# First row block on centered rows, its factor applied to the hidden units; fewer warm products, w1 loaded behind them

## The chip, the cores and the metric

The kernel runs on one core of a Trainium2 chip. The core has a matrix engine (TensorE, PE in the profile; the loading of its stationary operand is PEld), a vector engine (VectorE, DVE), a scalar engine for functions and copies (ScalarE, ACT), a fourth engine (GpSimd, POOL) and one that here only issues transfers (SyncE, SP). Each engine takes its instructions in the order written, and waits at one until its operands are there. Transfers between memory and the chip run on 16 DMA engines. The metric is the device time of the run in microseconds, as a median of several runs.

## The reference

x has 2048 rows of 640. The reference normalises each row, xn = (x - mean) / sqrt(var + 1e-5), and returns the sum of three things:

```python
a = jnp.einsum("bsd,ed->bse", xn, dft_hid_re)
b = jnp.einsum("bsd,ed->bse", xn, dft_hid_im)
y = jnp.einsum("ts,bse->bte", dft_seq_re, a) - jnp.einsum("ts,bse->bte", dft_seq_im, b)
h = gelu(jnp.einsum("bsd,df->bsf", xn, w1) + b1)      # 640 -> 1536, tanh form
m = jnp.einsum("bsf,fd->bsd", h, w2) + b2             # 1536 -> 640
return x + y + m
```

The part that the change touches is the first product of the two-layer network, xn times w1, for the first 512 rows.

## The kernel before

Every product is made in a split form: an operand is written as a high part in a rounded 32-bit format and a low part, the rest, and three products (high with high, high with low, low with high) stand for one. A split costs one copy on ScalarE (the high part, line 160) and one subtraction on VectorE (the low part, line 161).

The rows are worked on in blocks of 512 (`TB`). A hidden *unit* is 128 of the 1536 columns of w1, so a block has 12 units (`NF`). For a unit, `hidden(g)` (line 289) makes 5 x 3 products of 128x128 by 128x512 into one of three banks, `gelu(g, acc)` (line 310) applies bias and Gelu on ScalarE (314), copies the high part (318) and subtracts for the low part on VectorE (320), and `output(g)` (line 322) makes 5 x 3 products (lines 277 to 279) that add the unit's share to five output banks. The loop from line 1003 writes these out by hand: for the first block, at g, the weights of the next units are split (`prep_w1`, `prep_w2`), further ones are loaded, `first_block(i)` (886) does a piece of the normalising of later rows, and then come `hidden(g+2)`, `gelu(g+2)`, `output(g)`. The two-layer network of the later blocks and the Fourier part follow behind; nothing of them is changed.

Before the loop stands the head (lines 633 to 724), where nearly all of the waiting of TensorE for data lies. It loads four row tiles x0 to x3 of 128 rows (`load_x`, SP's queue), and then the weights in the same queue. VectorE zeroes a tile and casts it to three `warm` tiles. These lie in the three buffers that later hold the first three units of w1 (tag `w1r`), and so the load of a unit of w1 has to wait until the last product on the warm tile in its buffer is done. `NWARM` is the number of products on warm tiles, `NGATE` the numbers at which they go from one warm tile to the next: of 19, the first 7 use the first tile, 3 the second, the other 9 the third. Their result is not used.

Meanwhile the rows are normalised. The statistics of x0, x2 and x3 are made on VectorE (`ln_stats`, 185 and 186), of x1 on ScalarE (672 to 678). `ln_scale` (188) makes the factor, 1 / sqrt(var + eps): a Sqrt on ScalarE (192) and five small steps on VectorE. With mean and factor the rows are written, transposed in blocks of 32 columns, into `xp` (x0 and x1 on ScalarE, 686; x2 and x3 on VectorE, 208). TensorE transposes `xp` by 128x128 into five banks (`transpose_x`, 667), one for each 128 of the 640 columns; each bank takes a piece from each of the four row tiles. Five splits make the moving operands `XT[j]` of it. Between the rows, the first unit of w1 is split (706 and 711). `FIRST` (307) is the order of the 15 products of unit 0, by the column block j and the kind k (0 high-high, 1 high-low, 2 low-high): it follows the order in which the splits finish.

Some lines that a sentence can't say as shortly:

```python
NWARM = 19
NGATE = (7, 10)
    for k in range(NWARM):
        warm = warms[sum(k >= n for n in NGATE)]
        nc.tensor.matmul(wacc, warm[:, :P], warm, start=True, stop=True)
```

Of the kernel before, what the change touches and what calls it, by code (L numbers as in the profile page):

```python
# [19 lines left out]
NWARM = 19  # L20
NGATE = (7, 10)
TAIL = 4
PADL = 8
# [3 lines left out]
def kernel(  # L27
# [78 lines left out]
    def bank(k):  # L106
        return banks[:, k]
# [181 lines left out]
    def hidden(g):  # L289
# [9 lines left out]
        for n, (j, k) in enumerate(steps):  # L299
            a, b = kinds[k]  # L300
            nc.tensor.matmul(  # L301
                acc, W1[i][:, a, j * P : (j + 1) * P], XT[j][:, b], start=n == 0, stop=n == len(steps) - 1
            )
# [3 lines left out]
    FIRST = [(0, 0), (1, 0), (0, 2), (1, 2), (2, 0), (2, 2), (0, 1), (3, 0), (3, 2)]  # L307
    FIRST += [(1, 1), (4, 0), (4, 2), (2, 1), (3, 1), (4, 1)]

    def gelu(g, acc, fill=lambda k: None):  # L310

        i = unit(g)
        a = AB[:, g % 2]
        nc.scalar.activation(a, acc, AF.Gelu_apprx_tanh, bias=b1c[:, i : i + 1])
# [6 lines left out]

    def output(g):
        t, i = divmod(g, NF)
        if i == 0:
            oacc[t] = [bank(3 + e) for e in range(ND)]
        second(t, i, unit(g), HT[g])
# [305 lines left out]

    for c in range(NC):
        load_x(c)
    nc.gpsimd.memset(eps, EPS)
# [10 lines left out]
    for k in range(NWARM):  # L646
        warm = warms[sum(k >= n for n in NGATE)]
        nc.tensor.matmul(wacc, warm[:, :P], warm, start=True, stop=True)
    load_w1(2)
    load_w2(0)  # L650
    nc.sync.dma_start(b1c, b1.rearrange("(i p) -> p i", p=P))
    load_w2(1)
    load_w2(2)
# [16 lines left out]
    m = MV[:, 1]  # L670
    scratch = AB.rearrange("p a b -> p (a b)")
    nc.scalar.activation(scratch[:, :D], xt[1], AF.Copy, accum_out=m[:, 4:5])  # L672
    ln_stats(0)
    ln_scale(0, 1)
    nc.scalar.activation(m[:, 5:6], m[:, 4:5], AF.Copy, scale=-1.0 / D)
    nc.scalar.activation(scratch[:, :D], xt[1], AF.Square, bias=m[:, 5:6], accum_out=m[:, 2:3])
    nc.scalar.activation(m[:, 1:2], m[:, 2:3], AF.Copy, scale=1.0 / D)
    nc.scalar.activation(m[:, 0:1], m[:, 5:6], AF.Copy, scale=-1.0)

    def center(c):  # L680
        n = MV[:, c]
        nc.vector.scalar_tensor_tensor(n[:, 5:6], n[:, 0:1], -1.0, n[:, 3:4], op0=ALU.mult, op1=ALU.mult)

    def apply_on_act(c, j0, j1):
        n = MV[:, c]
        nc.scalar.activation(
            chunked(xp[:, c])[:, :, j0:j1],
            xt[c].rearrange("p (q c i) -> p q c i", q=Q, i=B)[:, :, j0:j1],
            AF.Identity,
            bias=n[:, 5:6],  # L690
            scale=n[:, 3:4],
        )

    center(0)
    apply_on_act(0, 0, ND)
    for c in (2, 3):
        ln_stats(c)
    transpose_x(0, 0, ND)
    ln_scale(1, 3)
    center(1)  # L700

    W1[0], first_w1 = slots[1, 0], w1r.pop(0).rearrange("p a b -> p (a b)")
    for j0, j1 in ((0, 2), (2, ND)):
        apply_on_act(1, j0, j1)
        if j0 == 0:
            nc.scalar.activation(W1[0][:, 0], first_w1, AF.Copy)
# [4 lines left out]
    nc.vector.tensor_tensor(W1[0][:, 1], first_w1, W1[0][:, 0].bitcast(F32), op=ALU.subtract)  # L711
# [8 lines left out]
    acc1 = hidden(1)  # L720
    prep_w2(0)
    prep_w1(2)
# [163 lines left out]
    def first_block(i):  # L886
# [116 lines left out]
    for g in range(NG):  # L1003
        t, i = divmod(g, NF)
        if t == 0:
# [4 lines left out]
            first_block(i)  # L1010
# [14 lines left out]
            else:  # L1025
                acc = hidden(g + 2)
# [5 lines left out]
                gelu(g + 2, acc)  # L1032
                output(g)
# [696 lines left out]
```

## Time and profile before

| | |
|---|---|
| median of 3 runs | 854.0 us (853.73 to 854.02) |
| the profiled execution | 853.7 us |
| its span, first to last instruction | 851.9 us |
| first warm product / last one's end | 1.92 / 8.43 us |
| first product of the first unit | 12.33 us |
| end of the 45 products of units 0 to 2 on the chain | 23.1 us |
| TensorE busy | 842.7 us (99%) |
| VectorE busy | 661.1 us (78%) |
| ScalarE busy | 353.6 us (42%) |

Times inside the profile count from the first instruction. A line of the timeline gives the start, the length, the engine, the line of the kernel, the operation, its output and inputs with their shapes and, in brackets, how long the engine was idle before it and what ended that; several like instructions in a row stand in one line with their number. The length of a matrix product in it holds the time until its result is out, so that two in a row overlap: how far apart they begin is what counts. The chain of waits goes back from the last instruction, at each step to what released it.

### The profile page before, as it was taken

How to read it: one execution, taken by the hardware profiler on the slowest of the kernel's cores; microseconds unless marked ns; L12 is line 12 of the kernel's file. 1: busy time of each engine (PE TensorE's matmuls, PEld its weight loads, DVE VectorE, ACT ScalarE, POOL GpSimd, SP SyncE). 2: the span in 40 equal slices, each digit the busy share in tenths (PEclk: the TensorE clock that was granted, in tenths of full speed). 3: DMA queues.
4: the chain of work that ended last, by engine and by line, in shares of the span. 5: the costliest groups of instructions: out<-in, count | busy, mean ns of one | idle time of the engine just before them, and what ended most of it. 6: DMA issues, size and time to landing. Idle time of an engine off the chain costs nothing.

```text
span 851.9 us, 10326 instructions
## 1 busy us (share of the span) xinstructions
PE 842.7 (99%) x3711; PEld 695.8 (82%) x3711; DVE 661.1 (78%) x836; ACT 353.6 (42%) x496; POOL 48.1 (6%) x69
## 2 busy tenths in 40 slices
PE   8999999999999999999999999999999999999997
PEld 6888888878888888888888888888888888888885
DVE  7554766785758888879979787889967998885686
ACT  7443634456666554343444343232323423222241
POOL 0000211031211300000000000000000000000001
PEclk9999999999999999999999999999999999999999
DMA  7757698937669998958744679663865779704464
GB/s 186 215 143 199 142 228 233 225 81 190 206 223 349 360 208 161 185 110 200 160 137 105 168 215 293 159 145 97 208 169 169 252 191 228 303 19 179 125 179 99
DMA packets 207235, 158.45 MB, mean 186 GB/s; under 512 B 80848, under 2 KB 180688, under 8 KB 206672
## 3 DMA queue, kind: packets, MB, share of 16 engines
q1 hardware_dynamic: 198880, 136.03, 62.6%
q0 software_dynamic: 4080, 20.97, 6.2%
q10 hardware_dynamic: 4224, 0.79, 0.4%
q8 instruction: 29, 0.48, 0.2%
q14 instruction: 22, 0.18, 0.1%
HBM read 114.76 MB, written 42.99 MB: 185 GB/s over the span
## 4 chain that ended last, share of the span: by engine, by line
PE 98%; DVE 1%; DMA 0%; ACT 0%; issue 0%; SPq 0%; ACTq 0%
PE banks L277 29%; PE banks L279 29%; PE banks L278 29%; PE banks L301 10%; DMA x<-in_A_x_dram 0%; PE banks L667 0%; DVE st L185 0%; ACT ab L672 0%; DVE yo L1695 0%; ACT mv L192 0%; DVE mv L186 0%; DVE xp L208 0%; SPq L178 0%; DVE mv L194 0%; DVE mv L196 0%
## 5 line engine op out<-in xcount | busy, mean ns | idle before, releaser
L277 PE MATMUL banks<-as,xab 128*128 128x512 f32 x411 | 159.9, 389 | 0.0
L279 PE MATMUL banks<-as,xab 128*128 128x512 f32 x411 | 159.9, 389 | 0.0
L278 PE MATMUL banks<-as,xab 128*128 128x512 f32 x411 | 159.9, 389 | 0.0
L160 ACT ACTIVATE as<-r 128x1024 fp32r<-128x1024 f32 x80 | 85.0, 1062 | 177.0 <-PE banks L279 149.2
L161 DVE TENSOR_TENSOR as<-r,as 128x1024 fp32r<-128x1024 f32 x80 | 97.2, 1216 | 41.7 <-ACT as L160 41.6
L278 PEld LDWEIGHTS banks<-as,xab 128*128 128x128 f32 x411 | 77.1, 188 | 16.1
L277 PEld LDWEIGHTS banks<-as,xab 128*128 128x128 f32 x411 | 77.1, 188 | 16.1
L279 PEld LDWEIGHTS banks<-as,xab 128*128 128x128 f32 x411 | 77.1, 188 | 16.0
L277 PE MATMUL banks<-as,xc 128*128 128x512 f32 x224 | 87.1, 389 | 0.0
L278 PE MATMUL banks<-as,xc 128*128 128x512 f32 x224 | 87.1, 389 | 0.0
L279 PE MATMUL banks<-as,xc 128*128 128x512 f32 x224 | 87.1, 389 | 0.0
L160 ACT ACTIVATE as<-rt 128x1024 fp32r<-128x1024 f32 x32 | 34.0, 1063 | 70.8 <-PE banks L279 62.8
L301 PE MATMUL banks<-xtt,xab 128*128 128x512 f32 x240 | 56.9, 390 | 0.0
L301 PEld LDWEIGHTS banks<-xtt,xab 128*128 128x128 f32 x240 | 45.0, 188 | 9.7 <-ACT xtt L160 0.5
L278 PEld LDWEIGHTS banks<-as,xc 128*128 128x128 f32 x224 | 42.0, 188 | 8.8
L279 PEld LDWEIGHTS banks<-as,xc 128*128 128x128 f32 x224 | 42.0, 188 | 8.8
L277 PEld LDWEIGHTS banks<-as,xc 128*128 128x128 f32 x224 | 42.0, 188 | 8.7
L161 DVE TENSOR_TENSOR as<-rt,as 128x1024 fp32r<-128x1024 f32 x32 | 38.8, 1212 | 5.3 <-ACT as L160 5.3
L320 DVE TENSOR_TENSOR hs<-ab,hs 128x512 fp32r<-128x512 f32 x24 | 17.6, 733 | 32.2 <-ACT hs L318 32.2
L160 ACT ACTIVATE as<-u 128x1024 fp32r<-128x1024 f32 (+1 forms) x24 | 22.1, 919 | 48.2 <-PE banks L279 48.2
L488 DVE STREAM_TRANSPOSE r<-raw 128x1024 f32<-128x1024 f32 x32 | 39.5, 1240 | 2.3 <-PE banks L279 1.8
L488 DVE STREAM_TRANSPOSE rt<-raw 128x1024 f32<-128x1024 f32 x32 | 38.8, 1230 | 0.9 <-PE banks L279 0.8
(336 smaller groups left out, 1618.2 us busy)
## 6 DMA issues: line engine op xcount, KB each, us to landing
raw<-in_A_dft_seq_re_dram SPq DMA_DIRECT2D x64, 256.0 KB, 5.8
raw<-in_A_dft_seq_im_dram SPq DMA_DIRECT2D x64, 256.0 KB, 5.1
ws<-wit SPq DMA_DIRECT2D x15, 384.0 KB, 4.1
x<-in_A_x_dram SPq DMA_DIRECT2D x16, 320.0 KB, 4.1
xs<-x SPq DMA_DIRECT2D x64, 80.0 KB, 1.8
xo<-in_A_x_dram SPq DMA_DIRECT2D x16, 320.0 KB, 6.4
xab<-wit SPq DMA_DIRECT2D x13, 384.0 KB, 4.3
wit<-wstp POOLq DMA_DIRECT2D x12, 384.0 KB, 3.9
```

Source lines behind the costliest of these rows:

```text
L160: nc.scalar.activation(h, s, AF.Copy)
L161: nc.vector.tensor_tensor(l, s, h.bitcast(F32), op=ALU.subtract)
L277: nc.tensor.matmul(acc, wh, mh, start=first, stop=False, skip_group_check=goes_on)
L278: nc.tensor.matmul(acc, wh, ml, start=False, stop=False, skip_group_check=goes_on)
L279: nc.tensor.matmul(acc, wl, mh, start=False, stop=last, skip_group_check=goes_on)
L301: nc.tensor.matmul(acc, W1[i][:, a, j * P : (j + 1) * P], XT[j][:, b], start=n == 0, stop=n == len(steps) - 1)
L320: nc.vector.tensor_tensor(hs[:, 1], a, hs[:, 0].bitcast(F32), op=ALU.subtract)
L488: nc.vector.transpose(held(pieces[g][2], u).rearrange("p c (n i) -> p c n i", i=B), r.rearrange("p n (c i) -> p c n i", i=B))
```

## The change

Instead of normalised rows, the first block uses centered rows, x - mean. They are transposed and split in place of the normalised ones. The factor of each row is a number for each of the 512 columns of a unit's bank, and it is multiplied onto the unit ahead of bias and Gelu. For that a tile `RB` with the factors along its columns, the same in all 128 partitions, is made: ScalarE spreads the four columns of factors to 4 x 128 columns (`wide`), TensorE transposes these four blocks into a bank (`spread`, called in `hidden(2)` behind the first of its products, `ASIDE = 1`), and ScalarE copies the bank to `RB`. Units 1 to 11 of the first block get a multiplication with `RB` on VectorE ahead of their Gelu; unit 0 is copied out of its bank, multiplied with the spread bank itself, and its Gelu reads that.

- The mean of x1 and x3 comes from a sum on ScalarE (`sum_on_act`), of x0 and x2 from the statistics on VectorE as before. x1 is centered on ScalarE, x0, x2 and x3 on VectorE. The variances of x1 and x3 are made later from the centered rows (`square_on_act`), and the factor of all four tiles by one `ln_scale(0, NC)`, behind the first two units in the order written.
- Warm products: 8 instead of 19, of which 4 use the first tile and 4 the second, and one more, on the third tile, behind the transposes of x0 and x1. So the first unit of w1 is loaded behind 4 products, the second behind 8, the third behind those transposes.
- `FIRST` has another order; the split of w1's unit 2 is written out ahead of its product; the Gelu table is asked for by a small activation ahead of the first Gelu.
- The first unit's output products (`first_output`) go through all five banks with the high part of the unit, and then through them with its low part.
- In the loop, `first_block(8)` (the transposing of the next block's first columns and the statistics of x8 and x9) is called behind the unit's Gelu; the statistics of x10 and x11 go behind the Gelu of the next turn.

```diff
@@ -17,9 +17,10 @@
 Q = 4
 B = 32
 EPS = 1e-5
-NWARM = 19
-NGATE = (7, 10)
+NWARM = 8
+NGATE = (4, 8)
 TAIL = 4
+ASIDE = 1
 PADL = 8
 
 
@@ -286,7 +287,7 @@
     def unit(g):
         return g if g < NF else LATE[g % NF]
 
-    def hidden(g):
+    def hidden(g, aside=None):
         i = unit(g)
         acc = bank(g % 3)
         kinds = ((0, 0), (0, 1), (1, 0))
@@ -297,6 +298,8 @@
 
             steps.sort(key=lambda s: s[1] == 2)
         for n, (j, k) in enumerate(steps):
+            if aside and n == ASIDE:
+                aside()
             a, b = kinds[k]
             nc.tensor.matmul(
                 acc, W1[i][:, a, j * P : (j + 1) * P], XT[j][:, b], start=n == 0, stop=n == len(steps) - 1
@@ -304,13 +307,18 @@
         return acc
 
 
-    FIRST = [(0, 0), (1, 0), (0, 2), (1, 2), (2, 0), (2, 2), (0, 1), (3, 0), (3, 2)]
-    FIRST += [(1, 1), (4, 0), (4, 2), (2, 1), (3, 1), (4, 1)]
+    FIRST = [(0, 0), (0, 2), (1, 0), (1, 2), (0, 1), (2, 0), (2, 2), (1, 1), (3, 0), (3, 2)]
+    FIRST += [(2, 1), (4, 0), (4, 2), (3, 1), (4, 1)]
 
     def gelu(g, acc, fill=lambda k: None):
 
         i = unit(g)
         a = AB[:, g % 2]
+        if g == 0:
+            acc = a
+        elif g < NF:
+            nc.vector.tensor_tensor(a, acc, RB, op=ALU.mult)
+            acc = a
         nc.scalar.activation(a, acc, AF.Gelu_apprx_tanh, bias=b1c[:, i : i + 1])
         fill(0)
         hs = HS[:, g % 3]
@@ -319,11 +327,27 @@
         fill(1)
         nc.vector.tensor_tensor(hs[:, 1], a, hs[:, 0].bitcast(F32), op=ALU.subtract)
 
+    def first_output(hs):
+        w = W2[0]
+        for k in range(2):
+            for e in range(ND):
+                cols = slice(e * P, (e + 1) * P)
+                if k == 0:
+                    nc.tensor.matmul(oacc[0][e], w[:, 0, cols], hs[:, 0], start=True, stop=False)
+                    nc.tensor.matmul(oacc[0][e], w[:, 1, cols], hs[:, 0], start=False, stop=False)
+                else:
+                    nc.tensor.matmul(
+                        oacc[0][e], w[:, 0, cols], hs[:, 1], start=False, stop=False, skip_group_check=True
+                    )
+
     def output(g):
         t, i = divmod(g, NF)
         if i == 0:
             oacc[t] = [bank(3 + e) for e in range(ND)]
-        second(t, i, unit(g), HT[g])
+        if g == 0:
+            first_output(HT[g])
+        else:
+            second(t, i, unit(g), HT[g])
 
     def second(t, i, u, hs, es=range(ND)):
         for e in es:
@@ -630,8 +654,14 @@
 
     warms = [early.tile([P, TB], F32R, tag="w1r", bufs=3, name=f"warm{k}") for k in range(3)]
 
+    RB = rows.tile([P, TB], F32, tag="yt", bufs=2, name="rb")
+
     for c in range(NC):
         load_x(c)
+    for tag, size, keys in PLACES:
+        t = whole[tag] = place(tag, (P, size // 4))
+        for k, key in enumerate(keys):
+            slots[key] = t[:, k * 2 * D : (k + 1) * 2 * D].rearrange("p (a b) -> p a b", a=2)
     nc.gpsimd.memset(eps, EPS)
     make_identity(nc, ident)
     nc.vector.memset(zeros, 0.0)
@@ -643,72 +673,67 @@
     load_w1(1)
 
     wacc = bank(0)
-    for k in range(NWARM):
+
+    def warm_up(k):
         warm = warms[sum(k >= n for n in NGATE)]
         nc.tensor.matmul(wacc, warm[:, :P], warm, start=True, stop=True)
+
+    for k in range(NWARM):
+        warm_up(k)
+    for j in range(ND):
+        new_xt(0, j)
+    tacc = [bank(3 + j) for j in range(ND)]
+
+    xp = out_pool.tile([P, NC, D], F32, tag="zo", bufs=1, name="xp")
+
+    def transpose_x(c, j0, j1):
+        for j in range(j0, j1):
+            nc.tensor.transpose(tacc[j][:, c * P : (c + 1) * P], xp[:, c, j * P : (j + 1) * P], ident)
+
+
+    scratch = AB.rearrange("p a b -> p (a b)")[:, :D]
+
+    def sum_on_act(c):
+        nc.scalar.activation(scratch, xt[c], AF.Copy, scale=-1.0 / D, accum_out=MV[:, c, 5:6])
+
+    def square_on_act(c):
+        nc.scalar.activation(scratch, xp[:, c], AF.Square, scale=D**-0.5, accum_out=MV[:, c, 1:2])
+
+    def center(c, op, shift, j0=0, j1=ND):
+        nc.vector.tensor_scalar(
+            chunked(xp[:, c])[:, :, j0:j1],
+            xt[c].rearrange("p (q c i) -> p q c i", q=Q, i=B)[:, :, j0:j1],
+            shift,
+            None,
+            op0=op,
+        )
+
+    W1[0], first_w1 = slots[1, 0], w1r.pop(0).rearrange("p a b -> p (a b)")
+
+    sum_on_act(1)
+    nc.scalar.activation(
+        chunked(xp[:, 1]), xt[1].rearrange("p (q c i) -> p q c i", q=Q, i=B), AF.Identity, bias=MV[:, 1, 5:6]
+    )
+    ln_stats(0)
+    center(0, ALU.subtract, MV[:, 0, 0:1])
+    ln_stats(2)
+    center(2, ALU.subtract, MV[:, 2, 0:1])
+    sum_on_act(3)
+    center(3, ALU.add, MV[:, 3, 5:6], 0, 2)
+    center(3, ALU.add, MV[:, 3, 5:6], 2, ND)
+    nc.scalar.activation(W1[0][:, 0], first_w1, AF.Copy)
+    nc.vector.tensor_tensor(W1[0][:, 1], first_w1, W1[0][:, 0].bitcast(F32), op=ALU.subtract)
+    transpose_x(0, 0, ND)
+    transpose_x(1, 0, ND)
+    warm_up(NWARM)
     load_w1(2)
     load_w2(0)
     nc.sync.dma_start(b1c, b1.rearrange("(i p) -> p i", p=P))
     load_w2(1)
     load_w2(2)
-
-    for tag, size, keys in PLACES:
-        t = whole[tag] = place(tag, (P, size // 4))
-        for k, key in enumerate(keys):
-            slots[key] = t[:, k * 2 * D : (k + 1) * 2 * D].rearrange("p (a b) -> p a b", a=2)
-    for j in range(ND):
-        new_xt(0, j)
-    tacc = [bank(3 + j) for j in range(ND)]
-
-    xp = out_pool.tile([P, NC, D], F32, tag="zo", bufs=1, name="xp")
-
-    def transpose_x(c, j0, j1):
-        for j in range(j0, j1):
-            nc.tensor.transpose(tacc[j][:, c * P : (c + 1) * P], xp[:, c, j * P : (j + 1) * P], ident)
-
-
-    m = MV[:, 1]
-    scratch = AB.rearrange("p a b -> p (a b)")
-    nc.scalar.activation(scratch[:, :D], xt[1], AF.Copy, accum_out=m[:, 4:5])
-    ln_stats(0)
-    ln_scale(0, 1)
-    nc.scalar.activation(m[:, 5:6], m[:, 4:5], AF.Copy, scale=-1.0 / D)
-    nc.scalar.activation(scratch[:, :D], xt[1], AF.Square, bias=m[:, 5:6], accum_out=m[:, 2:3])
-    nc.scalar.activation(m[:, 1:2], m[:, 2:3], AF.Copy, scale=1.0 / D)
-    nc.scalar.activation(m[:, 0:1], m[:, 5:6], AF.Copy, scale=-1.0)
-
-    def center(c):
-        n = MV[:, c]
-        nc.vector.scalar_tensor_tensor(n[:, 5:6], n[:, 0:1], -1.0, n[:, 3:4], op0=ALU.mult, op1=ALU.mult)
-
-    def apply_on_act(c, j0, j1):
-        n = MV[:, c]
-        nc.scalar.activation(
-            chunked(xp[:, c])[:, :, j0:j1],
-            xt[c].rearrange("p (q c i) -> p q c i", q=Q, i=B)[:, :, j0:j1],
-            AF.Identity,
-            bias=n[:, 5:6],
-            scale=n[:, 3:4],
-        )
-
-    center(0)
-    apply_on_act(0, 0, ND)
-    for c in (2, 3):
-        ln_stats(c)
-    transpose_x(0, 0, ND)
-    ln_scale(1, 3)
-    center(1)
-
-    W1[0], first_w1 = slots[1, 0], w1r.pop(0).rearrange("p a b -> p (a b)")
     for j0, j1 in ((0, 2), (2, ND)):
-        apply_on_act(1, j0, j1)
-        if j0 == 0:
-            nc.scalar.activation(W1[0][:, 0], first_w1, AF.Copy)
-        for c in (2, 3, 1):
-            if c != 1:
-                ln_apply_chunked(xp[:, c], c, j0, j1)
-            transpose_x(c, j0, j1)
-    nc.vector.tensor_tensor(W1[0][:, 1], first_w1, W1[0][:, 0].bitcast(F32), op=ALU.subtract)
+        transpose_x(2, j0, j1)
+        transpose_x(3, j0, j1)
     for j in range(ND):
         split(XT[j][:, 0], XT[j][:, 1], tacc[j])
     load_w1(3)
@@ -718,8 +743,30 @@
     acc0 = hidden(0)
     prep_w1(1)
     acc1 = hidden(1)
+
+    nc.gpsimd.tensor_scalar(MV[:, 1::2, 0], MV[:, 1::2, 5], -1.0, None, op0=ALU.mult)
+    square_on_act(1)
+    square_on_act(3)
+    ln_scale(0, NC)
+    W1[2] = slots[1, 2]
+    raw2 = w1r.pop(2).rearrange("p a b -> p (a b)")
+    nc.scalar.activation(W1[2][:, 0], raw2, AF.Copy)
+    nc.scalar.activation(AB[:, 0], acc0, AF.Copy)
+    wide = AB[:, 1]
+    nc.scalar.activation(
+        wide.rearrange("p (c n) -> p c n", c=NC), MV[:, :, 3:4].broadcast_to([P, NC, P]), AF.Copy
+    )
+    nc.vector.tensor_tensor(W1[2][:, 1], raw2, W1[2][:, 0].bitcast(F32), op=ALU.subtract)
+    nc.scalar.activation(eps[:, 1:2], eps[:, 0:1], AF.Gelu_apprx_tanh)
+
+    def spread():
+        for c in range(NC):
+            nc.tensor.transpose(bank(7)[:, c * P : (c + 1) * P], wide[:, c * P : (c + 1) * P], ident)
+
+    acc2 = hidden(2, spread)
+    nc.vector.tensor_tensor(AB[:, 0], AB[:, 0], bank(7), op=ALU.mult)
+    nc.scalar.activation(RB, bank(7), AF.Copy)
     prep_w2(0)
-    prep_w1(2)
     load_w2(3)
     load_w1(5)
 
@@ -901,8 +948,9 @@
                 load_x(c)
         if i in (8, 9):
             transpose_z(1, i - 8)
-            ln_stats(2 * i - 8)
-            ln_stats(2 * i - 7)
+        if i == 8:
+            ln_stats(8)
+            ln_stats(9)
         if i == 10:
             load_xo(0)
             ln_scale(8, 4)
@@ -1007,7 +1055,8 @@
             prep_w2(i + 1)
             load_w1(i + 6)
             load_w2(i + 4)
-            first_block(i)
+            if i != 8:
+                first_block(i)
             if i == NF - 1:
                 open_w()
                 acc = hidden(g + 2)
@@ -1023,13 +1072,18 @@
                 output(g)
                 gelu(g + 2, hidden(g + 2))
             else:
-                acc = hidden(g + 2)
+                acc = hidden(g + 2) if g else acc2
                 if i == NF - 3:
                     for j in range(ND):
                         prep_xt(1, j)
                         if j + 2 < ND:
                             transpose_z(1, j + 2)
                 gelu(g + 2, acc)
+                if i == 8:
+                    first_block(i)
+                if i == 9:
+                    ln_stats(10)
+                    ln_stats(11)
                 output(g)
         elif i < NF - 2:
             acc = hidden(g + 2)
```

More of the change, by code (lines that the diff above doesn't have):

```diff
@@ L712 @@
+    transpose_x(0, 0, ND)
+    transpose_x(1, 0, ND)
+    warm_up(NWARM)
+    load_w1(2)
+    load_w2(0)
+    nc.sync.dma_start(b1c, b1.rearrange("(i p) -> p i", p=P))
+    load_w2(1)
+    load_w2(2)
+    for j0, j1 in ((0, 2), (2, ND)):
+        transpose_x(2, j0, j1)
+        transpose_x(3, j0, j1)
     for j in range(ND):
```

5 lines of the change are left out of this document (removed).

## The prediction

> **What bounds the kernel now.** I read the page first, then the chain of waits in order of time over the first 24 us, then the head instruction by instruction (the timeline), then the stretches of TensorE.
>
> ```profile
> span 851.9 us, 10326 instructions
> PE 842.7 (99%) x3711; PEld 695.8 (82%) x3711; DVE 661.1 (78%) x836; ACT 353.6 (42%) x496; POOL 48.1 (6%) x69
> PE 98%; DVE 1%; DMA 0%; ACT 0%; issue 0%; SPq 0%; ACTq 0%
> ```
>
> ```profile
> 0.74 0.41 SPq L178
> ...
> 1.21 3.28 DMA x<-in_A_x_dram
> ...
> 4.51 0.83 ACT ab L672 x2
> ...
> 6.50 0.81 DVE st L185 x2
> ...
> 7.33 0.21 DVE mv L186
> ...
> 8.63 0.31 ACT mv L192
> ...
> 9.85 0.42 DVE xp L208
> ...
> 10.32 2.08 PE banks L667 x15
> 12.40 10.70 PE banks L301 x45
> ```
>
> The first fence says that the chain is TensorE for 98% of the span. The second shows the other part, the way to the first hidden product at 12.4: x1 lands (4.5), its sum, statistics of x2 and x3 (to 8.5), the factor (Sqrt at 8.63, five small steps on VectorE), the normalised rows (9.85), transposes (10.32). From there TensorE runs without a pause.
>
> ```profile
> 1.92:3.63 1.71, 1.71 (x4) 1.00 0.93 322
> 3.63:5.33 1.70, 1.70 (x5) 1.00 0.94 334
> 5.33:6.19 0.86, 0.86 (x3) 1.00 0.50 197
> 12.33:15.90 3.57, 3.57 (x15) 1.00 0.98 224
> 15.90:22.70 6.80, 6.80 (x31) 1.00 0.67 164
> ```
>
> These are stretches of TensorE alone (from:to, length, busy, instructions that touch the stretch, clock, DMA). The two hidden units from 15.90 take 6.80 us for 30 products (one of the 31 is cut by the edge): 0.227 us each, and so to the end. The first unit took 3.57 us instead of 3.40, held by the splits that make its operands. Before 5.33 a warm product took 0.427 us (4 in 1.71), in the next stretch 0.29: the array reached full speed only after 5.33, some 3.4 to 4.3 us after the first product. The clock column says 1.00 all along, so here the cadence is the witness. Since TensorE never pauses later, a microsecond gained or lost ahead of the second hidden unit moves the end by a microsecond, and work on other engines costs nothing while it stays ahead.
>
> **The change, part by part.**
>
> ```profile
> 3.77 0.89 DVE L185 BATCH_NORM_STATS2 st<-x 128x6 f32<-128x320 f32 x2 [1.23 <-DMA x<-in_A_x_dram]
> 4.51 0.74 ACT L672 ACTIVATE ab<-x 128x640 f32<-128x640 f32 x1 [2.28 <-DMA x<-in_A_x_dram]
> 5.15 0.19 ACT L672 ACTIVATION_READ_ACCUMULATOR ab<-x 128x1 f32 x1
> 5.30 5.61 SPq L255 DMA_DIRECT2D w1r<-in_B_w_dram  x12
> 5.65 0.83 ACT L676 ACTIVATE ab<-x,mv 128x640 f32<-128x640 f32 x1
> 6.80 0.91 ACT L686 ACTIVATE xp<-x,mv 128x640 f32<-128x640 f32 x1
> 8.27 0.71 PE L667 MATMUL banks<-ident,xp 128*128 128x128 f32 x5
> 9.85 1.51 DVE L208 TENSOR_SCALAR xp<-x,mv 128x256 f32<-128x256 f32 x4
> 10.48 0.72 ACT L706 ACTIVATE xab<-w1r 128x640 fp32r<-128x640 f32 x1
> 11.28 0.82 DVE L711 TENSOR_TENSOR xab<-w1r,xab 128x640 fp32r<-128x640 f32 x1
> 11.70 2.52 ACT L160 ACTIVATE xtt<-banks 128x512 fp32r<-128x512 f32 x5
> 12.31 3.08 DVE L161 TENSOR_TENSOR xtt<-banks,xtt 128x512 fp32r<-128x512 f32 x5 [0.21 <-ACT xtt L160]
> 16.12 1.28 ACT L314 ACT_TABLE_LOAD   x1
> 17.41 0.69 ACT L314 ACTIVATE ab<-banks,b1c 128x512 f32<-128x512 f32 x1
> 18.13 0.63 ACT L318 ACTIVATE hs<-ab 128x512 fp32r<-128x512 f32 x1
> ```
>
> ```profile
> L178 SPq DMA_DIRECT2D x<-in_A_x_dram x4: 407/420/432, 0.7 to 2.1; - x4
> DMA to landing us min/median/max: 3.0/3.6/4.3
> ```
>
> ```profile
> DMA to landing us min/median/max: 1.9/2.1/2.1
> ```
>
> (The timeline: start, length, engine, line; then the four issues of x with their time to landing; then that time for the first four pieces of w1.)
>
> *Centering instead of normalising.* x0 lands at 0.74 + 3.0 = 3.74, x1 at 4.49, x3 at 2.1 + 4.3 = 6.4, and x2, from the median of the four, near 5.6. VectorE: statistics of x0 3.77 to 4.9 (0.89 and an aggregate of 0.21), centering to 5.55 (640 columns at the rate of the 256 and 384 of L208, some 0.65), statistics of x2 5.65 to 6.8, centering to 7.45. ScalarE: sum of x1 4.51 to 5.34, shift 5.37 to 6.28 (0.91, as L686), sum of x3 6.44 to 7.27 (0.74 and the read of 0.19). VectorE centers x3 in pieces, 7.45 to 7.85 and to 8.2. TensorE needs 4 transposes for the first two banks after 7.85: they are full at about 8.15. Removed from this path: Sqrt, reciprocal and Newton steps (8.63 to 9.85) and the queue of statistics behind x0's own factor.
>
> *w1 sooner.* Its first load waits for 4 warm products instead of 7: at 0.427 us that is 1.92 + 4 x 0.427 + 0.4 of drain (the last of seven ended 5.3, 0.4 past its successor's start) = 4.0 instead of 5.30. SP then issues four pieces at 0.47 each (5.61 for 12), so the last at 5.4, and lands 2.1 later: 7.5. It may be pushed by x3, which is still moving until 6.4. Bounds: 7.2 (2.0 after issue, nothing in the way) and 8.3 (x3's last 0.9 us in full ahead of it). I take 7.5, nearest the rows. The high half of w1 on ScalarE then ends 8.2, the low half on VectorE 9.05. SP holds nothing else that is early: w1's second unit goes behind the first (issued by 7.9, landed near 10, used at 10.5), w2 and the bias follow earlier than before. The third unit of w1 waits for the ninth product, behind x1's transposes, at some 7.4: SP arrives at 7.9, so nothing queued behind it (w2, the bias) is held; its split is wanted at 13.4.
>
> *First unit.* The first split starts on ScalarE at 8.2 and takes as long as in the row 11.70 to 12.33: the first product stands at 8.8 instead of 12.33. Splits then come every 0.48 on ScalarE (2.52 for 5) and 0.6 on VectorE (3.08 for 5). The new order of the 15 products uses two per ScalarE split, with the low halves behind; followed product by product it ends 3.6 us later, as the row 12.33:15.90 had it. So the second unit begins at 12.4 instead of 15.9: **-3.5 us**.
>
> *Spread.* Four transposes go into the third unit, behind its first product: 4 x 0.109 (row 8.27: five of them 0.109 apart with one tail of 0.27) = **+0.44 us** on the bound engine. They wait for the factor: ScalarE after the splits (10.7) has the second w1 (0.64 apart), two squares with their reads (0.92 each), Sqrt 0.3 to 13.4; VectorE's arithmetic 0.9 to 14.3; ScalarE meanwhile makes w1 of the third unit and saves the first unit's sum, then the wide copy of the factor at about 14.4 to 15.1. TensorE arrives at 12.4 + 3.4 + 0.23 = 16.0. So 0.9 us to spare; without it each 1 us is paid in full. The Gelu table (1.28) is fetched beside that. POOL has one small operation more (the means of x1 and x3), long before the stores that use it. The rest to the first output: multiply 0.7, Gelu 0.69, copy 0.63, with one w2 split (0.72) between, ready at 18.9, against an arrival at 12.4 + 6.8 + 0.44 = 19.6. 0.7 us to spare; the reordered first output needs only the high half there, the low half 2.3 us later.
>
> *A multiply on each of the other units.* Eleven multiplies of a bank (some 0.69, as one of L161's) ahead of Gelu. Behind its wait for TensorE stand on VectorE the low half of that unit, the next w1 and w2 splits and the statistics; waiting for them are the output two units later and the unit after.
>
> ```profile
> 29.93 0.69 ACT L314 ACTIVATE ab<-banks,b1c 128x512 f32<-128x512 f32 x1 [4.19 <-PE banks L301]
> 84.10:90.90 6.80, 6.80 (x31) 5.63 (x30) 6.63 (x14) 2.13 (x4) 0.00 (x0) 1.00 0.00 2
> ```
>
> The first row says that in a period of 6.80 us (unit and output) ScalarE stood idle 4.19 us for TensorE: 0.7 more in that loop is hidden, cost nothing.
> The second is the stretch with the fullest VectorE (6.63 of 6.80, the third busy figure), where block 1's rows are transposed and split: there one multiply is added behind the splits, and the statistics of two row tiles (four of 0.41 to 0.49 and two aggregates of 0.21) are moved behind it, so the splits come sooner, not later. What stands behind those statistics is the next factor and its stores; they were, and are, wanted only in block 1. I take **0**; bounds: -0.1 (nothing there is on the bound engine) and +1.5 (two multiplies that find no gap).
>
> *Warm products.* Nine instead of 19. They lie beside the loads and cost nothing themselves; what they buy is the clock. Eight end their cadence at 1.92 + 3.41 = 5.33; the row 5.33:6.19 has the speed change after that, with products still running. So whether the array is at full speed at 8.8 is open. Bounds: 0, and the whole wait again from 8.8. By the rows a wait of 3.4 to 4.3 us, say 4; each us at half speed loses 1 - 0.227/0.427 = 0.47, thus 1.9, of which 0.3 is won back because the first unit then waits for no split: +1.6. I take 0, because the pauses between 5.33 and 8.8 are filled with 20 transposes and a product, and because in this trace the array kept its full speed over 8.43 to 12.33 with only 20 transposes in it (0.109 apart at 10.3 too). For the other end speaks the row 5.33:6.19 itself. [...]
>
> **Sum.** -3.5 + 0.44 = -3.1 us. The profiled execution took 853.7 us (span 851.9 and 1.8 around it), so 850.6; the median of the runs is 0.3 above it, and I say 850.9.
>
> **The rivals.**
> *The clock comes late.* The last paragraph's price: 850.9 + 1.6 = 852.5, between 851.9 and 854 as the change of speed falls. For it: speed rose only after 5.33. Against: no pause on TensorE before 8.8 is over 1 us. [...]
>
> *Start or factor a microsecond late.* Six steps on three engines end at 8.8 and the spread has 0.9 us to spare; if x3 and w1 share the DMA engines (0.93 to 0.94 busy up to 5.33) w1 lands at 8.3 and x3 half a us late, so +0.8 to 1.0; or a small step of the factor waits on ScalarE's longer queue and TensorE stands at the spread. Then the change does only part of what it says: 851.9.
>
> [...]
>
> **How the numbers follow.** What a measurement of this kernel can tell from no change is about 0.2%, or 1.7 us: faster means below 852.3, slower above 855.7. Forecast 0.55 (all faster). Late clock 0.20 (0.03 of it faster, the rest the same). Late start or factor 0.13 (0.10 faster, 0.03 same). Slower 0.12. Together 0.68 faster, 0.20 same, 0.12 slower. The likeliest is 850.9; its own range goes from 849.8 (w1 at 7.2, spread half hidden, no other price) to 851.8. The range takes in the late clock and the late start and leaves out the slower case: 849.8 to 854.6.
>
> **What would show it.** In the profile after: the first hidden product at 8.8 (8.4 to 9.6) instead of 12.33, and the second unit's first at 12.4; the high half of w1 on ScalarE at 7.5, waiting on its load or on nothing; the gap of the first unit's products at 0.23, not 0.43 (if 0.43, the clock rival is right and its end is the time of the change); no idle time of TensorE ahead of the four transposes into the last bank and none ahead of the first output; units 6.80 us apart with their outputs as before through the block; block 1's first unit without a pause. A pause of TensorE at any of these places makes the time longer by just that much.

## The result, and the profile after

The changed kernel takes 852.75 us (median of 22 runs, 851.89 to 854.2) against 854.0 us (22 runs, 853.62 to 855.06): a ratio of 0.9985, 95% interval 0.9979 to 0.9991. It is faster by 0.15%, or some 1.25 us, where 3.1 us were forecast; by the bound of 0.2% set in the prediction that counts as the same. The profiled execution took 852.8 us.

The page of the changed kernel, the lines that answer to those of before:

```profile
span 851.0 us, 10311 instructions
PE 842.0 (99%) x3705; PEld 694.7 (82%) x3705; DVE 667.2 (78%) x838; ACT 355.1 (42%) x498; POOL 48.7 (6%) x70
PE 97%; ACT 1%; DVE 1%; DMA 0%; issue 0%; SPq 0%; ACTq 0%; DVEq 0%
```

TensorE's timeline over the head (start, length, engine, line; the number of products at the end; in brackets what it waited for):

```profile
1.91 3.78 PE L679 MATMUL banks<-warm 128*128 128x512 f32 x8 [1.91 <-DVE warm L669]
5.71 1.97 PE L691 MATMUL banks<-ident,xp 128*128 128x128 f32 x10
...
8.40 1.09 PE L691 MATMUL banks<-ident,xp 128*128 128x128 f32 x8 [0.26 <-DVE xp L703]
9.64 7.53 PE L304 MATMUL banks<-xtt,xab 128*128 128x512 f32 x31
17.01 0.60 PE L764 MATMUL banks<-ident,ab 128*128 128x128 f32 x4
17.36 3.46 PE L304 MATMUL banks<-xtt,xab 128*128 128x512 f32 x14
20.99 0.50 PE L336 MATMUL banks<-hs,rt 128*128 128x512 f32 x1 [0.16 <-ACT hs L326]
21.33 0.40 PE L337 MATMUL banks<-hs,rt 128*128 128x512 f32 x1
...
24.52 2.84 PE L304 MATMUL banks<-xtt,xab 128*128 128x512 f32 x10
```

And the chain of waits of the same stretch:

```profile
5.35 2.91 DMA w1r<-in_B_w_dram
...
8.36 0.74 ACT xab L724
9.10 0.49 ACT xtt L161
...
9.64 7.53 PE banks L304 x31
17.17 0.45 PE banks L764 x4
...
17.72 0.70 DVE ab L767
...
18.44 0.60 ACT rb L768
19.04 0.63 ACT rt L161
19.66 0.62 ACT ab L322
...
20.30 0.64 ACT hs L326
...
20.97 0.69 DVE hs L328
21.66 0.61 DVE ab L320
...
22.30 0.73 ACT ab L322
...
23.59 0.73 ACT xab L161
...
24.34 0.84 DVE xab L162
...
25.23 1.90 PE banks L304 x7
```

The head is shorter: the first hidden product stands at 9.64 us instead of 12.33. But three things are new in the chain. Its way to that product goes over the last piece of w1, which lands at 5.35 + 2.91 = 8.26. Between the spread (17.17) and the first output (20.99) it leaves TensorE and runs over VectorE's multiply, ScalarE's copy of the factors, a split of w2, Gelu and copy. From there it does not come back to TensorE at once: beside the first output's products it goes on over the low half of unit 0 (20.97), the added multiply of unit 1 (21.66), that unit's Gelu and the split of unit 3's w1, whose low half (24.34 to 25.18) ends after TensorE has come to it.

What this adds up to in the profiled executions, from the starts of the products (the product before the first output starts at 20.44, the one before the pause in unit 3 at 24.76; without a pause the next starts 0.227 later):

| place | us |
|---|---|
| first hidden product, 12.33 to 9.64 | -2.69 |
| first unit, 3.80 to 3.70 | -0.10 |
| third unit with the spread, 3.40 to 3.90 | +0.50 |
| pause ahead of the first output, 0.32, and the restart behind it, 0.11 | +0.43 |
| pause in unit 3, 0.25, and its restart, 0.11 | +0.36 |
| sum | -1.50 |

The last product of all starts 1.37 us sooner (the last row of TensorE, before and after):

```profile
845.55 0.39 PE L279 MATMUL banks<-as,xab 128*128 128x512 f32 x1
```

```profile
844.18 0.39 PE L280 MATMUL banks<-as,xab 128*128 128x512 f32 x1
```

The span shrank by 0.9 only, because in this execution the stores behind the last product took 6.4 us and not 6.0; in the further profiles of this kernel they took 6.0.

### The profile page after: what moved, and what is told of

Same layout as the page of the kernel before. It is cut to its first block, busy times and chain, and to the rows that moved or that the text cites. A ratio compares the mean times of both kernels' runs of the same rounds, so it can differ in the third digit from the quotient of the medians.

```text
span 851.0 us, 10311 instructions
## 1 busy us (share of the span) xinstructions
PE 842.0 (99%) x3705; PEld 694.7 (82%) x3705; DVE 667.2 (78%) x838; ACT 355.1 (42%) x498; POOL 48.7 (6%) x70
## 3 DMA queue, kind: packets, MB, share of 16 engines
q0 software_dynamic: 4080, 20.97, 6.2%
## 4 chain that ended last, share of the span: by engine, by line
PE 97%; ACT 1%; DVE 1%; DMA 0%; issue 0%; SPq 0%; ACTq 0%; DVEq 0%
PE banks L279 29%; PE banks L278 29%; PE banks L280 29%; PE banks L304 9%; DMA w1r<-in_B_w_dram 0%; PE banks L679 0%; ACT ab L322 0%; SPq L256 0%; DVE xab L162 0%; ACT xab L724 0%; ACT xab L161 0%; DVE yo L1749 0%; DVE ab L767 0%; DVE hs L328 0%; ACT hs L326 0%
## 5 line engine op out<-in xcount | busy, mean ns | idle before, releaser
L162 DVE TENSOR_TENSOR as<-u,as 128x1024 fp32r<-128x1024 f32 (+1 forms) x24 | 24.9, 1042 | 18.8 <-ACT as L161 18.8
```

The costliest lines, as they stand in the source:

```text
L162: nc.vector.tensor_tensor(l, s, h.bitcast(F32), op=ALU.subtract)
```

## The experiments

The theory after the comparison: the start is late because x3 and w1 share the DMA engines; two pauses come from the order of work on ScalarE and VectorE; the clock is up in time. Rivals: the clock is late in part of the executions; the extra multiply or the late statistics hold back the later rows, and with them the loads of a later stage. The runs below were made on three chips, on which the kernel before took 853.81, 853.84 and 853.86 us. The changed kernel and the new order ran on two of them. The versions without the multiplications, with 12 products in the new order, and with 4 products ran on the third, so these three are compared across chips. Medians of 6 to 11 runs scatter by some tenths of a microsecond, and a profile is of one execution only.

**The changed kernel again**, twice, to compare with.

> The changed kernel unchanged, beside the others on one chip. Every theory expects 852.0 to 853.5 us, 0.6 to 2 us below the kernel before. Its profile is a second look at the head: the theory that loads collide expects x3 to land near 7.1 us again and the first hidden product near 9.6; the theory that the clock comes late in part of the executions would show 0.43 us between the products of the first unit in some profile.

> The changed kernel once more, to compare the others with. 852.4 to 853.2 us by every theory; its profile is a third look at when x3 and w1 land (7.1 and 8.0 to 8.3 if the loads collide each time).

852.87 us (11 runs) and 852.82 us (11 runs). x3 landed at 7.11 and 7.01, the last piece of the first w1 at 8.02 and 8.17, the first product stood at 9.42 and 9.55. In the second profile TensorE ended 1.54 us sooner than before, in agreement with the table. The first profile (853.35 us) has a pause that the others lack. Its VectorE waited longer for a store of the other weights. Against the profile under the result, VectorE was 2 us late ahead of this wait, 4.1 us at its end and still 1.1 us at 179, where TensorE waits behind it. The rows are VectorE's of this execution and the pause, and then the same wait in the profile under the result:

```profile
154.65 0.81 DVE L162 TENSOR_TENSOR wst<-wt,wst 128x256 fp32r<-128x256 f32 x2 [4.02 <-DMA wit<-wst]
...
181.83 0.50 PE L278 MATMUL banks<-xtt,tw 128*128 128x512 f32 x1 [1.27 <-ACT banks L857]
```

```profile
150.52 0.81 DVE L162 TENSOR_TENSOR wst<-wt,wst 128x256 fp32r<-128x256 f32 x2 [1.84 <-DMA wit<-wst]
```

So a gain at the head can be taken back near 180 us when that store is slow. Why it is slow in some executions was not settled.

**First load of w1 behind 6 warm products.**

```diff
-NGATE = (4, 8)
+NGATE = (6, 8)
```

> The first unit of w1 is loaded behind 6 warm products instead of 4 (0.85 us later). Theory of colliding loads: x3 lands at 6.4 to 6.6 us again instead of 7.1, the last piece of w1 at 8.2 to 8.5 us although it was issued 0.85 us later, and the time stays within 0.3 us of the changed kernel. Rival, each load takes its own fixed time: x3 still lands at 7.1, w1 at 9.1, and the time is 0.8 us longer than that of the changed kernel.

852.70 us, within 0.2 us of the changed kernel beside it. The issues of x and of w1 with their times to landing, first of the changed kernel, then of this one:

```profile
L179 SPq DMA_DIRECT2D x<-in_A_x_dram x4: 398/420/432, 0.7 to 2.1; - x4
DMA to landing us min/median/max: 3.1/3.8/5.0
```

```profile
DMA to landing us min/median/max: 2.7/3.1/3.3
```

```profile
L179 SPq DMA_DIRECT2D x<-in_A_x_dram x4: 403/422/432, 0.7 to 2.1; - x4
DMA to landing us min/median/max: 3.0/3.6/4.5
```

```profile
DMA to landing us min/median/max: 2.1/2.2/2.7
```

The longest x is x3: 5.0 us against 4.5 (and 4.3 before), and a piece of w1 needs 2.2 us instead of 3.1. The loads do slow each other down, and the other profiles agree: x3 landed at 6.4 us in the kernel before, where w1 is issued from 5.3 on, at 6.6 here, and at 7.0 to 7.6 in six profiles with the loads of the changed kernel, from 4.0. w1's last piece, issued 0.85 us later, landed only 0.44 us later, at 8.70, a little past what was expected. In this one execution the first product stood at 10.07, later than in any of the changed kernel's; the median does not show it.

**Order around the spread.** The split of w2's first unit is taken apart, and the Gelu of unit 0 goes ahead of the copy of the factors:

```diff
+    W2[0] = slots[2, 0]
+    raw_first = w2r.pop(0).rearrange("p (q c i) -> p q c i", q=Q, i=B)
+    nc.scalar.activation(chunked(W2[0][:, 0]), raw_first, AF.Copy)
     def spread():
...
     nc.vector.tensor_tensor(AB[:, 0], AB[:, 0], bank(7), op=ALU.mult)
+    nc.vector.tensor_tensor(
+        chunked(W2[0][:, 1]), raw_first, chunked(W2[0][:, 0]).bitcast(F32), op=ALU.subtract
+    )
+    gelu(0, acc0)
     nc.scalar.activation(RB, bank(7), AF.Copy)
-    prep_w2(0)
...
-    gelu(0, acc0)
     gelu(1, acc1)
```

> Only the order on ScalarE and VectorE around the spread is changed: the high half of w2's first unit is copied ahead of the spread, and the Gelu of unit 0 goes ahead of the copy of the factors out of the bank. Theory that the two pauses of TensorE (0.32 us ahead of the first output, 0.25 us in unit 3, each with 0.11 us at the restart) come from ScalarE standing idle behind VectorE's read of the spread bank: both pauses go, 0.7 to 0.8 us shorter than the changed kernel. Rival, the pauses come from a late load or from the factor itself: one or both stay and the time changes by less than 0.3 us.

> The reordered version once more, beside the changed kernel on the same chip. Theory of the two pauses: 0.7 to 0.8 us below the changed kernel; the 1.5 us seen the first time would then be half chance. Rival, that the order does nothing and the first result was chance: within 0.3 us of the changed kernel.

851.38 us and 851.47 us (6 runs each), 1.49 and 1.35 us below the changed kernel beside them; ratios to the kernel before 0.9972 (0.9961 to 0.9984) and 0.9970 (0.9958 to 0.9982). Both pauses are gone. A late load was not their cause: w2's first unit had landed at 13.2 us in the changed kernel, unit 3's w1 at 17.1. The waits of the changed kernel show where the time went: ScalarE stood 1.2 us ahead of its copy of the spread bank (768). Some 0.4 of it is the wait for the spread itself, which ends at 17.6; the other 0.7 is VectorE's read of the same bank (767), behind which the copy was ordered.

```profile
ACT rb L768 <- DVE ab L767: 1.2, 1, 1.2
```

ScalarE in the second run of this version does the w2 copy in that time (17.30), and then Gelu, the high half, and only then the copy of the factors:

```profile
17.30 0.72 ACT L764 ACTIVATE rt<-w2r 128x640 fp32r<-128x640 f32 x1
18.60 0.73 ACT L322 ACTIVATE ab<-ab,b1c 128x512 f32<-128x512 f32 x1 [0.58 <-DVE ab L771]
19.36 0.63 ACT L326 ACTIVATE hs<-ab 128x512 fp32r<-128x512 f32 x1
19.89 0.58 ACT L776 ACTIVATE rb<-banks 128x512 f32<-128x512 f32 x1
```

and TensorE goes on without a pause from the third unit into the first output and into unit 3:

```profile
17.52 3.47 PE L304 MATMUL banks<-xtt,xab 128*128 128x512 f32 x14
20.83 0.39 PE L336 MATMUL banks<-hs,rt 128*128 128x512 f32 x1
...
24.23 1.07 PE L304 MATMUL banks<-xtt,xab 128*128 128x512 f32 x4
```

The new order moves the copy of w2 ahead and the copy of the factors back in one edit, so the share of each is not shown. The two pauses account for 0.79 us. The profiles agree with that: from the first hidden product to the last of all, the changed kernel takes 834.5 us where it has no pause near 180, the second run of this version 833.6. So do the fastest executions: 851.9 us in each of the three runs of the changed kernel, 851.0 in both of this one. The other half microsecond between the medians is not explained; the first profile of this version itself has a pause of 0.57 us near 670, behind a load of weights, so such pauses come and go. Of the versions that leave nothing out this is the fastest.

**The multiplications left out** in the reordered version. Units 1 to 11 of the first block are then computed without the factor.

```diff
-        elif g < NF:
-            nc.vector.tensor_tensor(a, acc, RB, op=ALU.mult)
-            acc = a
```

> The reordered version (the w2 copy ahead of the spread, Gelu of unit 0 ahead of the copy of the factors) with the multiplications of units 1 to 11 by the factor left out, so that these units are computed without the factor of their rows; all else stays. Theory that the extra multiply, with VectorE's wait behind it, holds back the normalising of later rows and so the stores and loads on which a pause of TensorE near 180 us hangs: the stores of x8 to x11 start 1 to 2 us sooner than 94.9, the pause near 180 shrinks from 0.3 to 0.1 or none, and the time is 0.2 to 0.8 us below the reordered version. Rival, the multiply is hidden: the same time within 0.2 us.

851.29 us (7 runs): within 0.2 us of the reordered version. SP's stores of x8 to x11 did start sooner, at 93.60 instead of 94.91 (first this one, then the reordered version), but near 180 two products still begin 0.30 us apart. That is the "pause" of 0.3 of the expectation: 0.07 us more than 0.227, in the kernel before and in the changed one alike. So in the new order the multiply is hidden, and the rival that it holds back the later stages falls.

```profile
93.60 4.55 SPq L204 DMA_DIRECT2D xs<-x  x10
```

```profile
94.91 3.13 SPq L204 DMA_DIRECT2D xs<-x  x7
```

**The late statistics alone**, in the kernel before.

```diff
         if i in (8, 9):
             transpose_z(1, i - 8)
-            ln_stats(2 * i - 8)
-            ln_stats(2 * i - 7)
+        if i == 8:
+            ln_stats(8)
+            ln_stats(9)
...
-            first_block(i)
+            if i != 8:
+                first_block(i)
...
                 gelu(g + 2, acc)
+                if i == 8:
+                    first_block(i)
+                if i == 9:
+                    ln_stats(10)
+                    ln_stats(11)
                 output(g)
```

> The kernel before, with one part of the change alone: the transposing and the statistics of x8 and x9 behind the Gelu of that turn, the statistics of x10 and x11 behind the next Gelu. Theory that this part costs nothing by itself: stores of x8 to x11 at 96.3 us give or take 0.5, the pause near 182 as before (0.3 us), 854.0 within 0.3 us. Rival, that it is this part that holds back the stores and loads: stores 1 to 2 us later, the pause near 182 at 1 us or more, 854.8 us or more.

853.95 us (11 runs) beside 853.84 of the kernel before, ratio 1.0001 (0.9992 to 1.0010). The stores start at 95.35 us here and at 96.29 in the kernel before:

```profile
95.35 3.60 SPq L203 DMA_DIRECT2D xs<-x  x8
```

This part costs nothing by itself.

**12 warm products**, in the changed kernel and in the reordered version.

```diff
-NWARM = 8
+NWARM = 12
```

> 12 warm products ahead of the transposes instead of 8, so that TensorE is busy without a pause up to 7 us; the gates of w1 stay. Theory that the clock is up in time in the changed kernel: within 0.3 us of it, the same scatter. Rival, the clock is late in part of its executions: 0.5 to 1.5 us shorter in the median and the scatter of the single times (2.3 us in the changed kernel) down to about 1 us.

> The reordered version with 12 warm products ahead of the transposes instead of 8. If the clock comes late in part of the executions with 8: 0.4 to 0.6 us below the reordered version (851.4), scatter under 1.2 us. If the 0.6 us seen between 8 and 12 products without the reordering were chance, or came of the loads' collisions: 851.4 again within 0.3 us, with the first hidden product at 9.4 to 9.9.

852.28 us, 0.59 us below the changed kernel beside it, with a scatter of 1.1 us (851.93 to 853.02), as the rival of the late clock had it; and then 852.41 us on the reordered version, about 1 us above its two medians. The signs contradict each other, so neither shows that 8 products are too few. In both profiles x3 landed late (7.6 and 7.4 us) and the first product came at 9.91 and 9.71; the second also has a pause of 0.57 us near 180.

**4 warm products.**

```diff
-NWARM = 8
-NGATE = (4, 8)
+NWARM = 4
+NGATE = (4, 4)
```

> The changed kernel with 4 warm products instead of 8, all on the first tile (the first load of w1 waits for the same 4; the second no longer waits for a warm product). [...]

853.61 us (11 runs), ratio to before 1.0002 (0.9993 to 1.0011), some 0.8 us above the changed kernel. Seven of its times lie between 852.7 and 853.6 us, four between 854.6 and 855.6. The edit did more than was meant. With no product on the second warm tile, the first load of w1 no longer waited for the products: SP issued it at 2.60 us, not at 4.01, and x3 landed at 7.62. So this version differs from the changed kernel in the loads too, and how much of its 0.8 us comes of the clock is not shown. The profile is of its fastest execution: SP's issues of w1, a row of TensorE's timeline, then two stretches with the number of instructions that touch them (10 transposes begin in the first, 6 in the second).

```profile
2.60 7.67 SPq L256 DMA_DIRECT2D w1r<-in_B_w_dram  x12
5.69 2.37 PE L691 MATMUL banks<-ident,xp 128*128 128x128 f32 x10 [1.71 <-DVE xp L703]
```

```profile
5.69:7.82 2.13, 2.13 (x11) 1.00 1.11 282
9.30:9.96 0.66, 0.66 (x8) 1.00 0.41 123
```

In the first stretch transposes begin 0.213 us apart, in the second 0.109. TensorE had run no warm product between 4.0 and 7.7 us, and only one then; all the same full speed was there by 9.30, ahead of the first unit at 10.05. In the four long executions it may have come later still; no profile shows one of them.

**x1 and x3 issued from ScalarE's queue**, in the reordered version.

```diff
     for c in range(NC):
-        load_x(c)
+        load_x(c, nc.scalar if c % 2 else nc.sync)
```

> The reordered version with x1 and x3 issued from ScalarE's queue, so that the four loads of x are issued within 0.5 us of each other and not over 1.8. Theory that the head ends late because x3 is still under way when w1's pieces start: x3 lands by 6.2 to 6.5 us, w1 by 7.5 to 7.8, the first hidden product at 8.8 to 9.1 as the prediction had it, the time 0.4 to 0.8 us below the reordered version beside it. Rival, the DMA engines are full from 2 us on and the issue does not matter: x3 at 7.0 and the time of the reordered version within 0.3 us.

851.89 us (11 runs; five from 850.75 to 851.22, five from 852.58 to 853.4), ratio to before 0.9977 (0.9968 to 0.9985), so not below the reordered version in the median. x3 did what was expected: ScalarE began its sum at 6.29 us. w1 did not: it was there at 8.03 and not by 7.8, so it is not x3's late landing alone that holds it. And the profile, of the longest execution, shows the clock:

```profile
1.90 3.78 PE L679 MATMUL banks<-warm 128*128 128x512 f32 x8 [1.90 <-DVE warm L669]
6.40 2.37 PE L691 MATMUL banks<-ident,xp 128*128 128x128 f32 x10 [0.71 <-DVE xp L703]
8.42 0.78 PE L679 MATMUL banks<-warm 128*128 128x512 f32 x1
8.99 1.83 PE L691 MATMUL banks<-ident,xp 128*128 128x128 f32 x10
10.57 1.64 PE L304 MATMUL banks<-xtt,xab 128*128 128x512 f32 x6
```

x0 landed at 4.5 instead of 3.8, probably because it shared the engines with x1 to x3; TensorE stood 0.71 us behind the warm products; all ten first transposes ran at half speed, some 0.21 us apart (2.37 us against 1.97 in the changed kernel), most of the later ones too, 0.21 apart up to 10.05 and 0.11 from 10.22 on (1.83 us for ten, where the changed kernel took 1.09 for eight); and the first hidden product came at 10.57, 2.5 us behind the last load, where the changed kernel needs 1.4. But this execution lost time a second time, where TensorE waited for a load of other weights:

```profile
674.58 0.47 PE L278 MATMUL banks<-as,gr_b 128*128 128x512 f32 x1 [0.96 <-DMA gr_b<-wit]
```

This product starts 1.35 us behind the one before it. The last product of all comes 1.75 us later than in the second run of the reordered version: 0.76 is the later start, and most of the rest this pause. Which of the two divides the two groups of times is not shown.

**w1's first unit in one piece** of long rows, in the changed kernel. The data are rows of w2, so unit 0 is computed with other numbers.

```diff
+        if i == 0:
+            eng.dma_start(t.rearrange("p a b -> p (a b)"), w2[:P, :])
+            return
         v = w1.rearrange("(q c i) f -> q i c f", q=Q, i=B)
```

> The changed kernel with the load of w1's first unit replaced by one piece of the same size with long rows, taken from w2, so that units 0 and 10 are computed with other numbers. Theory that w1's four pieces of short rows set the start: that load lands at 7.0 to 7.3 us, the first hidden product comes at 9.0 to 9.3 with x3 as the next limit, and the time is 0.3 to 0.6 us below the changed kernel. Rival, that x3 alone sets the start: the first product stays at 9.4 to 9.7 and the time within 0.2 us.

852.26 us (11 runs), 0.56 us below the changed kernel beside it. The piece landed 3.8 us after its issue at 4.01, at 7.8, later than expected; x3 landed at 7.0, and the first product stood at 9.34. Both loads are close together at the limit: with w1 there sooner the first product comes some tenths sooner, and then x3 with its sum and centering is the next. The gain in the median is no larger than the 0.59 us that 12 products showed and then did not repeat.

## Why the prediction was right or wrong

- **The structure held.** TensorE bounds the kernel, the factor is off its path, and what the head gains shows at the end: the table's sum agrees with the last product of two profiles within 0.15 us. Direction and range were right; the size was 1.25 us instead of 3.1. The time lies outside the forecast's own range, 849.8 to 851.8, and inside the wide one only because that takes in two rivals; "the same" had been given 0.20. In the first profile the gap between 3.1 and 1.5 is 0.84 from the later start, 0.79 from the two pauses and 0.06 from the spread, less 0.10 in the first unit. That the late clock's price, 852.5, is nearest to the result is chance: the clock was up in time.
- **"w1 sooner" was mis-sized.** It took 7.5 for w1 and 6.4 for x3, and gave 8.3 as the bound if x3's data went ahead of w1's. Measured: 8.0 to 8.3 in three profiles, and x3 at 7.0 to 7.1. The two loads mix, so each delays the other: with w1 issued later, x3 landed at 6.4 and 6.6. That makes the first product 9.4 to 9.6 instead of 8.8, a cost of 0.6 to 0.8 us. This is the first half of the rival "start or factor a microsecond late", which had priced it at 0.8 to 1.0.
- **"First unit" misread a row by one product.** The unit took 3.80 us before, not 3.57: the stretch 12.33:15.90 ends as the last product starts. Both kernels have it, so the difference was not touched.
- **"Spread" was right in its first half.** It took 0.44 and cost 0.50, and TensorE did not wait for the factor. Its second half, "0.7 us to spare" ahead of the first output, failed: the sum had multiply, Gelu, copy and one w2 split, but not ScalarE's copy of the factors (0.60), nor that this copy, and with it the w2 split behind it, would wait for VectorE's read of the bank. Its own rows, one behind the other (16.0, 0.44, 0.7, 0.72, 0.69, 0.63), give 19.2 and not 18.9; with the copy it is 19.8, after the arrival at 19.6. Instead of 0.7 to spare there was a pause of 0.43 with its restart. The reordered version shows it by taking it away.
- **"A multiply on each of the other units" holds in the new order** (left out there, the time stays), but the paragraph named the next w1 split as waiting behind it and took its price as 0 from a period far into the block. In the changed kernel unit 1's multiply is 0.61 us of the chain to the second pause; no run shows whether that pause would go with the multiply alone. In unit 3, the first that is prepared behind all this, its low half ended at 25.18 us and was wanted at 24.98: 0.36 with the restart. The early units needed their own working.
- **The late statistics**, taken as 0, cost nothing: shown alone in the kernel before.
- **The clock**, taken as 0, was up before the first unit: in the profile under the result and in the second of the two further ones of the changed kernel, the 31 products from the first one on take 7.53 and 7.55 us, 0.24 each. None of its profiles is of an execution over 854 us. The traces' own record of the clock has full speed from 6.04 us in the kernel before, where warm products begin 0.427 us apart up to 5.93 and 0.227 from 6.45 on, and from 7.14 in the changed kernel, where transposes begin 0.213 us apart up to 7.02 and 0.109 from 7.19 on. It lasts 843.09 and 839.68 us there, past the last product. By the distance of the transposes it was there by 9.30 with 4 products and by 10.22 with two queues, both ahead of the first hidden product (10.05 and 10.57). (The clock column of the views says 1.00 even before that.) So the time of the rise moves by microseconds, but no profile shows the bound of +1.6. Nor does a run show the late clock's range, 851.9 to 854, as the price of a late rise: in the changed kernel the rise comes 2.5 us ahead of the first hidden product. The prediction's 0.29 us for a product in 5.33:6.19 counts one that began before: two begin there, 0.43 apart, and the speed rose 4.1 us after the first product, as "say 4" had it. Which work on TensorE brings the rise no run separates: with 4 warm products it ran 14 transposes and one product between 4.0 and 9.30 us, and was at full speed then.
- **Slower** did not come about: even with 4 warm products those of the first unit begin 0.25 us apart (8 in 2.13 us from 10.05 on), and the time is that of the kernel before.

## What to carry to other kernels

When a chain is taken off the path, write out the queue of each engine behind the new place in full, copies included, and look for two engines that read one bank: here 0.8 us of 3 went into waits that a change of order removed. Loads that are issued sooner can meet others that are still moving: here the first pieces of w1, issued from 4.01 us on instead of 5.30, took 2.7 to 3.3 us instead of 1.9 to 2.1, and x3 landed at 7.1 instead of 6.4. And when warm products are cut down, see in the profile when full speed comes: at 6.04 us with 19, at 7.14 with 8, and between 10.05 and 10.22 with the same number in the version with two queues, where the first load came late.

## What was not expected of the hardware

- Each of the two pauses of TensorE in the changed kernel cost 0.11 us more than itself: behind them the first two products begin 0.34 us apart instead of 0.227 (20.99 and 21.33, 25.23 and 25.57).
- Transposes of 128x128 in 32 bits begin 0.213 us apart below full speed and 0.109 at it, and with 4 warm products, where TensorE ran only 14 transposes and one product between 4.0 and 9.30 us, they stood at 0.109 from there on.
- The stores behind the last product took 6.0 us in the profile of the kernel before and 6.4 in that of the changed one; the difference is a third of the gain measured here.
